# Moving the batch-end sums of a fused attention, Fourier and feed-forward kernel between engines, with a tile of their own for the spread reciprocals

## The chip, the core and the metric

The kernel runs on one core of a Trainium2 chip. The core has five engines that run beside each other and meet at semaphores: TensorE (PE in the profile; PEld is its weight load), VectorE (DVE), ScalarE (ACT), GpSimd (POOL) and SyncE (SP), which here only starts transfers. Each takes its own instructions strictly in their order. The metric is the device time of one launch in microseconds.

## The reference, cut to what matters

Four batches of 576 rows; attention with 8 heads of 64 channels and a decay that is a running sum of logarithms; then the real part of a two-dimensional Fourier transform, added to its input; then a normalisation and a feed-forward pair; then a mixing stage with sines and cosines.

```python
scores = scale * q @ k.T + (cum[:, None] - cum[None, :])      # causal
attn = exp(scores - max); attn = attn / (attn.sum(-1) + 1e-9)
x = (attn @ v)                                                # 4 x 576 x 512
u = x + real(fft(fft(x, axis=1), axis=2))
x = u + relu(norm(u) @ w_ch1) @ w_ch2
theta = x @ w_theta
y = w_tok_r @ (x * cos(theta)) + w_tok_i @ (x * sin(theta))
u = x + y;  out = u + relu(u @ w_ch)
```

Products are done in a reduced format with each operand split into a high part and a low part, so that most tensors exist twice ("hi" and a low part, "kl", "el", "ol" and so on): a copy makes the high part, a subtraction the low part.

## The kernel before, in words

Phase 1 (`phase1`) walks over 32 heads, two of a batch's eight to a pair, four pairs to a batch. For head n+1 it computes scores (`score_units`: two matmuls into a bank, L232 on the high part and L233 on the low parts kl and the query copy q2; a fused VectorE reduction L241 that adds the mask and finds the lowest value; an exponential on ScalarE, L246). For head n it turns the probabilities (`turn_units`: transposes L271 into four banks, copied to PT at L274, bank 0 by VectorE and banks 1 to 3 by ScalarE). For head n+2 it prepares the operands (`prep_units`: ScalarE makes hi at L206, GpSimd the two low parts at L209 and L211 and the query copy at L213). After both heads of a pair come the product with v (`av_units`, L303, into a bank pair T) and the reciprocals of the row sums, turned by TensorE (`spread`, L283) and copied by ScalarE to a tile R (L285, L287).

`evac_pair` multiplies T by R. Before, R is the tile X for an even pair and the tile Y for an odd one (Y shares its memory with ol), and the product overwrites it. After each odd pair rows of Y are shifted by transfers through a small tile, and then the sum E = X + Y (L348) and the difference O = X - Y (L350) are formed: once in the middle of each batch (pair 1) and once at its end (pair 3). With the batch's end, `fft_units` follows: ee (L377) and oo (L381) fold E and O, ScalarE makes eh and oh, then el (L384) and ol (L386) are the low parts; matmuls L406, L417 and L429 with the tables in `dft`; and u at L446 and L447. This runs as filler in the steps of later heads; for the last batch it runs at the start of phase 2.

Phase 2 is the feed-forward pair (L745, L759) over six column blocks and sixteen weight groups; phase 3 the mixing stage. Weights arrive packed and are decoded by ScalarE and VectorE (`decode`, scratch tile a of the tag sq); phase 3 takes its z tiles from the same memory (`z_tile`).

The order on each engine of phase 1 is set by a scheduler that runs ahead of time: it takes the instructions in program order, with matmuls of the scores and of the product with v preferred (`high_priority`), and fixes one list for each engine. From the fifth column block of phase 2 on the order is the program's own.

Of the kernel before, what the change touches and what calls it, by code (L numbers as in the profile page):

```python
# [18 lines left out]
NP = 4  # L19
# [32 lines left out]
def f(ap):  # L52
    return ap.bitcast(F32)


class Net:
# [138 lines left out]
    def prep_units(self, n, pair, raw, hd):  # L195
        nc = self.nc
        g = n % 2
        kl, q2 = pair["kl"], self.q2[g]
        hi = self.w2.tile([128, 2, S], F32R, tag="hi", name="hi")
        hd["hi"] = hi  # L200
        if n == 0:
            nc.scalar.copy(hi[:, 1], raw[:, 1])
            nc.scalar.copy(hi[:, 0], raw[:, 0])
            nc.scalar.copy(q2[0:64], raw[0:64, 1])
        else:
            nc.scalar.copy(hi, raw)  # L206
        yield
        lows = nc.vector if n == 0 else nc.gpsimd
        lows.tensor_tensor(hi[64:128, 1], raw[64:128, 1], f(hi[64:128, 1]), ALU.subtract)  # L209
        yield  # L210
        lows.tensor_tensor(kl[0:64, g], raw[0:64, 0], f(hi[0:64, 0]), ALU.subtract)  # L211
        if n:
            nc.gpsimd.tensor_scalar(q2[0:64], raw[0:64, 1], 1.0, 1.0, ALU.mult, ALU.mult)  # L213
        yield
# [43 lines left out]
    def turn_units(self, hd):  # L258
        nc = self.nc
        P = hd["P"]  # L260
        PT = self.w3.tile([128, 1600], F32, tag="PT", name="PT", bufs=4)
        hd["PT"], hd["copies"] = PT, []
        for bank, pieces in enumerate(TURNED):
            ps = self.bank_b()
            for j, a, b, off in pieces:
                for i in range(5):
                    if TOP[i] + 128 <= a or TOP[i] >= b:
                        continue
                    o = off + TOP[i] - a
                    src = P[:, POFF[i] + TOP[j] : POFF[i] + TOP[j] + 128]  # L270
                    nc.tensor.transpose(ps[:, o : o + 128], src, self.ident)  # L271
            w = TWIDE[bank]
            dst = PT[:, PTOFF[bank] : PTOFF[bank] + w]
            copy = nc.scalar.copy(dst, ps[:, 0:w]) if bank else nc.vector.tensor_copy(dst, ps[:, 0:w])  # L274
            hd["copies"].append(copy)
            yield

    def spread(self, p, T, wide):
        nc = self.nc
        R = self.c1.tile([128, S], F32, tag="ol" if p % 2 else "X", name="Y" if p % 2 else "X", bufs=1)  # L280
        for ps, some in ((self.bank_b(), range(4)), (self.bank_a(), (4,))):
# [41 lines left out]

    def evac_pair(self, p, R, T):
        nc = self.nc
        k = p // 2
        if p % 2 == 0:
            self.X = R
            nc.vector.tensor_tensor(R, T[:, 256:832], R, ALU.mult)
            if k == 0:  # L330
                self.EO = [self.c1.tile([128, 2, S], F32, tag=x, name=x, bufs=2) for x in ("E", "O")]
            return
        X, (E, O) = self.X, self.EO
        Y = R
        nc.vector.tensor_tensor(Y, T[:, 256:832], R, ALU.mult)
        if k == 0:
# [9 lines left out]
        for _ in range(4):  # L346
            yield
        nc.vector.tensor_tensor(E[:, k], X, Y, ALU.add)  # L348
        yield
        nc.vector.tensor_tensor(O[:, k], X, Y, ALU.subtract)  # L350
        yield

    def fft_units(self, b, E, O, rows):
# [5 lines left out]
        for _ in rows:  # L359
            pass  # L360
        ee = w.tile([128, 2, 290], F32, tag="ee", name="ee", bufs=1)
        oo = w.tile([128, 2, 288], F32, tag="oo", name="oo", bufs=1)
# [13 lines left out]
        yield  # L376
        nc.vector.tensor_tensor(ee[:, :, 1:288], E[:, :, 1:288], E[:, :, 575:288:-1], ALU.add)  # L377
        nc.scalar.copy(ee[:, :, 0:289:288], E[:, :, 0:289:288])
        nc.scalar.copy(eh, ee)
        yield  # L380
        nc.vector.tensor_tensor(oo[:, :, 0:287], O[:, :, 1:288], O[:, :, 575:288:-1], ALU.subtract)  # L381
        nc.scalar.copy(oh, oo)
        yield
        (nc.gpsimd if 0 >> (b == B - 1) & 1 else nc.vector).tensor_tensor(el, ee, f(eh), ALU.subtract)  # L384
        yield
        (nc.vector if 3 >> (b == B - 1) & 1 else nc.gpsimd).tensor_tensor(ol, oo, f(oh), ALU.subtract)  # L386
        for _ in range(4):
# [44 lines left out]
        for t in range(2):  # L432
# [12 lines left out]
            nc.vector.scalar_tensor_tensor(oa[:, 289:576], O[:, t, 289:576], -0.5, ps[:, 287:0:-1], ALU.mult, ALU.subtract)  # L445
            (nc.vector if b == B - 1 or 1 >> t & 1 else nc.gpsimd).tensor_tensor(u[:, t, :], ea, oa, ALU.subtract)  # L446
            nc.gpsimd.tensor_tensor(u[:, 2 + t, :], ea, oa, ALU.add)  # L447
            for _ in range(1 if b == B - 1 or t else 7):
# [7 lines left out]
    def phase1(self):  # L456
# [16 lines left out]
        def done(m, T, R):  # L473
            nonlocal rows, fft
            for _ in rows:
                pass
            rows = self.evac_pair(m % NP, R, T)
            next(rows, 0)
# [62 lines left out]
    def decode(self, src, n, place=None, keep=None):  # L541
# [7 lines left out]
        yield  # L549
        a = w.tile([128, 512], F32, tag="sq", name="a", bufs=6)[:, 0:n]  # L550
        if keep is None:
# [338 lines left out]
    def z_tile(self):  # L890
        k = self.nz % 7
        self.nz += 1
        if k < 6:
            return self.x1.tile([128, 2, 256], F32R, tag="sq", name="z", bufs=6)
        return self.q3.tile([128, 2, 256], F32R, tag="z", name="z", bufs=1)

# [290 lines left out]
```

## Time and profile before

| | us |
|---|---|
| median of 3 runs | 980.65 (980.25 to 983.48) |
| profiled execution | 979.22 |
| its span, first to last instruction | 977.5 |
| PE busy | 910.4 (93%) |
| DVE busy | 620.3 (63%) |
| ACT busy | 431.1 (44%) |
| POOL busy | 330.8 (34%) |

The shares are means over three phases with different limits: phase 1 ends at about 290 us, phase 2 at about 700 us. In the page's 40 slices TensorE's busy tenths are 9 in every slice from the 17th to the 39th, and 4 to 9 ahead of them. In a row of the profile a line number is that of the kernel before; the names are those of the program, output first. "PEclk" is the clock granted to TensorE as a share of full speed (2.4 GHz; its lower level is 1.2 GHz, a share of 0.5).

### The profile page before, as it was taken

To read this page: it belongs to the slowest core of one execution; us is meant where nothing else is said; L and a number is where in the kernel's file an instruction comes from. 1 tells how busy PE (TensorE), PEld (TensorE's weight loads), DVE (VectorE), ACT (ScalarE), POOL (GpSimd) and SP (SyncE) were. 2 spreads that over 40 slices of the span, in tenths; PEclk is the share of its full clock that TensorE was granted. 3 is DMA by queue.
4 is the path that set the end of the run, shared out by engine and by line. 5 is a ranking of instruction groups with operands and counts; after the bars stand their busy time and mean duration, and the time that the engine had idled before them with its cause. 6 is when DMAs were issued, how large, how long until landed. Compare 5 with 4: busy or idle time off the path is not lost.

```text
span 977.5 us, 15831 instructions
## 1 busy us (share of the span) xinstructions
PE 910.4 (93%) x5960; PEld 855.0 (87%) x5960; DVE 620.3 (63%) x1464; ACT 431.1 (44%) x1038; POOL 330.8 (34%) x385
## 2 busy tenths in 40 slices
PE   4889898987978998999999999999999999999998
PEld 3677776776757898999999999999999999999998
DVE  7666667576669787625665366626677765746554
ACT  5888668667554343312322133213335543525331
POOL 6867467467531253300000000000014744525330
PEclk9999899988988799999999999999999999999999
DMA  4643232222022212001223122232420000000001
GB/s 144 198 156 102 87 101 88 91 73 88 15 84 68 65 65 66 1 1 45 86 87 118 55 87 87 89 130 92 144 68 1 1 14 37 2 37 14 25 26 49
DMA packets 24337, 68.04 MB, mean 70 GB/s; under 512 B 3535, under 2 KB 6991, under 8 KB 24261
## 3 DMA queue, kind: packets, MB, share of 16 engines
q1 hardware_dynamic: 20420, 62.52, 19.7%
q0 software_dynamic: 3120, 3.33, 1.3%
q10 hardware_dynamic: 720, 1.18, 0.4%
q8 instruction: 47, 0.77, 0.3%
q14 instruction: 30, 0.24, 0.1%
HBM read 57.92 MB, written 9.07 MB: 69 GB/s over the span
## 4 chain that ended last, share of the span: by engine, by line
PE 68%; DVE 15%; ACT 7%; POOL 5%; issue 4%; DMA 2%; SPq 0%; ACTq 0%; POOLq 0%; DVEq 0%
PE pa L745 19%; PE pb L759 11%; PE po L759 8%; PE pb L966 5%; PE pa L977 4%; PE pa L930 4%; PE pt L303 3%; PE po L966 3%; PE pb L271 2%; PE pa L232 2%; ACT P L246 2%; PE pa L233 2%; ACT hi L206 1%; DVE P L241 1%; PE pb L429 1%
## 5 line engine op out<-in xcount | busy, mean ns | idle before, releaser
L745 PE MATMUL pa<-un,wf 128*128 128x384 f32 x1152 | 222.0, 340 | 5.1 <-ACT un L733 3.2
L745 PEld LDWEIGHTS pa<-un,wf 128*128 128x128 f32 x1152 | 203.8, 191 | 7.8 <-ACT un L733 3.9
L751 DVE SCALAR_TENSOR_TENSOR h<-pa,h 128x384 fp32r<-128x384 f32 x96 | 53.2, 555 | 145.6 <-ACT h L750 145.5
L759 PE MATMUL pb<-h,wf 128*128 128x384 f32 x660 | 135.2, 337 | 0.3 <-DVE u L767 0.3
L759 PEld LDWEIGHTS pb<-h,wf 128*128 128x128 f32 x660 | 117.0, 189 | 0.6 <-DVE u L767 0.6
L750 ACT ACTIVATE h<-pa 128x384 fp32r<-128x384 f32 x96 | 46.8, 489 | 154.7 <-PE pa L745 154.6
L246 ACT ACTIVATE P<-P,mn 128x256 f32<-128x256 f32 (+4 forms) x160 | 95.7, 601 | 40.9 <-DVE mn L241 40.7
L241 DVE CUSTOM_DVE_ANT_0 P<-pa,mask 128x256 f32<-128x256 f32 (+4 forms) x160 | 78.3, 512 | 55.5 <-PE pa L233 45.4
L759 PE MATMUL po<-h,wf 128*128 128x384 f32 x492 | 104.4, 340 | 1.1 <-DVE u L767 0.8
L232 PE MATMUL pa<-hi 128*128 128x448 f32 (+2 forms) x192 | 73.6, 396 | 27.7 <-DVE mn L241 11.9
L922 POOL COPY xd<-u 128x64 f32<-128x64 f32 x32 | 6.7, 251 | 272.0 <-DVE u L767 263.8
L966 PE MATMUL pb<-wtk,z 128*128 128x288 f32 x513 | 97.0, 294 | 0.0
L271 PE MATMUL pb<-ident,P 128*128 128x128 f32 x480 | 86.1, 292 | 9.4 <-ACT PT L274 6.2
L759 PEld LDWEIGHTS po<-h,wf 128*128 128x128 f32 x492 | 87.3, 189 | 2.8 <-ACT a L558 1.1
L956 POOL TENSOR_TENSOR z<-kra,z 128x256 fp32r<-128x256 f32 x72 | 53.8, 767 | 86.8 <-ACT z L955 86.8
L966 PEld LDWEIGHTS pb<-wtk,z 128*128 128x128 f32 x513 | 79.2, 188 | 0.0
L966 PE MATMUL po<-wtk,z 128*128 128x288 f32 x351 | 75.1, 295 | 1.1 <-POOL z L956 1.1
L271 PEld LDWEIGHTS pb<-ident,P 128*128 128x128 f32 x480 | 60.6, 148 | 17.0 <-ACT PT L274 9.1
L233 PE MATMUL pa<-kl,q 66*128 66x448 f32 (+2 forms) x192 | 67.1, 372 | 7.0 <-POOL kl L211 3.9
L232 PEld LDWEIGHTS pa<-hi 128*128 128x128 f32 x192 | 39.6, 209 | 37.5 <-DVE mn L241 15.4
L930 PE MATMUL pa<-wf,xs 128*128 128x256 f32 x456 | 63.9, 289 | 0.0
L966 PEld LDWEIGHTS po<-wtk,z 128*128 128x128 f32 x351 | 57.4, 188 | 1.7 <-POOL z L956 1.5
(203 smaller groups left out, 1692.7 us busy)
## 6 DMA issues: line engine op xcount, KB each, us to landing
raw<-in_qk SPq DMA_DIRECT2D x31, 576.0 KB, 3.9
raw<-in_wf SPq DMA_DIRECT2D x32, 512.0 KB, 3.5
raw<-in_wtk SPq DMA_DIRECT2D x18, 288.0 KB, 2.8
v<-in_vp SPq DMA_DIRECT2D x16, 320.0 KB, 3.5
out<-ob SPq DMA_DIRECT2D x12, 288.0 KB, 2.1
dft<-in_dft POOLq DMA_DIRECT2D x8, 346.0 KB, 5.0
raw<-in_wth SPq DMA_DIRECT2D x4, 512.0 KB, 4.6
st_wth<-raw SPq DMA_DIRECT2D x4, 512.0 KB, 5.0
```

What stands on the lines that cost most here:

```text
L232: nc.tensor.matmul(t[:, 0 : b - a], hi[:, 1, q], hi[:, 0, a:b], start=True, stop=False)
L233: nc.tensor.matmul(t[:, 0 : b - a], q2[:, q], kl[:, g, a:b], start=False, stop=True)
L241: nc.vector.tensor_tensor_reduce(out=p[:, a:b], in0=t[:, 0 : b - a], in1=self.mask[:, S - n0 - 128 + a : S - n0 - 128 + b], scale=-0.125, ...
L246: nc.scalar.activation(p, p, AF.Exp, bias=lowest, scale=-1.0, accum_out=zs[:, g, i : i + 1])
L271: nc.tensor.transpose(ps[:, o : o + 128], src, self.ident)
L745: nc.tensor.matmul(ps[:, 0:CH], t[:, l, 128 * d : 128 * d + 128], un[r][:, d], start=n == 0, stop=n == 11)
L750: nc.scalar.activation(h[:, 0], ps[:, 0:CH], AF.Relu)
L751: nc.vector.scalar_tensor_tensor(h[:, 1], ps[:, 0:CH], 0.0, f(h[:, 0]), ALU.max, ALU.subtract)
L759: nc.tensor.matmul(outs[d], t[:, l, 128 * d : 128 * d + 128], h[:, r], start=k % G == 0 and n == 0, stop=k % G == G - 1 and n == 2,)
L930: nc.tensor.matmul(th, xs[:, l, d], self.wth[d][:, r, 256 * hf : 256 * hf + 256], start=n == 0, stop=n == 11)
L956: nc.gpsimd.tensor_tensor(z[:, 1], t, f(z[:, 0]), ALU.subtract)
L966: nc.tensor.matmul(acc[k][th], z[:, l, 128 * k : 128 * k + 128], self.wtk[kt][:, r, 288 * th : 288 * th + 288], start=first and i == 0 and ...
```

## The change

1. `spread` writes to a tile R of its own, and `evac_pair` writes its product to X or Y, instead of multiplying in place.
2. In `evac_pair` E and O go from VectorE to GpSimd, except at the end of the last batch; a step of the schedule is put in behind each.
3. In `fft_units` ee, oo, el, ol and both u go through one name, `two`: GpSimd for the first three batches, VectorE for the last. Before, ee, oo, el and ol were VectorE's in all batches, L446 VectorE's at t = 0 and GpSimd's at t = 1 (VectorE's twice in the last batch), L447 GpSimd's in all.
4. The query copy q2 goes from GpSimd to ScalarE for all heads but the first, where it was there already, and stands before the low parts.
5. Bank 1 of the turned probabilities is copied by VectorE instead of ScalarE.
6. To make room, `decode` has 5 scratch tiles a instead of 6; z tiles come 5 from that memory and 2 from another instead of 6 and 1.

```diff
         else:
             nc.scalar.copy(hi, raw)
         yield
+        nc.scalar.copy(q2[0:64], raw[0:64, 1])
         lows = nc.vector if n == 0 else nc.gpsimd
         lows.tensor_tensor(hi[64:128, 1], raw[64:128, 1], f(hi[64:128, 1]), ALU.subtract)
         yield
         lows.tensor_tensor(kl[0:64, g], raw[0:64, 0], f(hi[0:64, 0]), ALU.subtract)
-        if n:
-            nc.gpsimd.tensor_scalar(q2[0:64], raw[0:64, 1], 1.0, 1.0, ALU.mult, ALU.mult)
         yield
...
-            copy = nc.scalar.copy(dst, ps[:, 0:w]) if bank else nc.vector.tensor_copy(dst, ps[:, 0:w])
+            copy = nc.scalar.copy(dst, ps[:, 0:w]) if bank > 1 else nc.vector.tensor_copy(dst, ps[:, 0:w])
...
     def spread(self, p, T, wide):
-        R = self.c1.tile([128, S], F32, tag="ol" if p % 2 else "X", name="Y" if p % 2 else "X", bufs=1)
+        R = self.c1.tile([128, S], F32, tag="R", name="R", bufs=1)
...
-    def evac_pair(self, p, R, T):
+    def evac_pair(self, p, R, T, last):
         nc = self.nc
         k = p // 2
-        if p % 2 == 0:
-            self.X = R
-            nc.vector.tensor_tensor(R, T[:, 256:832], R, ALU.mult)
+        odd = p % 2
+        Z = self.c1.tile([128, S], F32, tag="ol" if odd else "X", name="Y" if odd else "X", bufs=1)
+        nc.vector.tensor_tensor(Z, T[:, 256:832], R, ALU.mult)
...
-        nc.vector.tensor_tensor(E[:, k], X, Y, ALU.add)
-        yield
-        nc.vector.tensor_tensor(O[:, k], X, Y, ALU.subtract)
+        sums = nc.vector if last else nc.gpsimd
+        sums.tensor_tensor(E[:, k], X, Y, ALU.add)
+        yield
+        yield
+        sums.tensor_tensor(O[:, k], X, Y, ALU.subtract)
+        yield
         yield
...
+        two = nc.vector if b == B - 1 else nc.gpsimd
...
-        nc.vector.tensor_tensor(ee[:, :, 1:288], E[:, :, 1:288], E[:, :, 575:288:-1], ALU.add)
+        two.tensor_tensor(ee[:, :, 1:288], E[:, :, 1:288], E[:, :, 575:288:-1], ALU.add)
...
-        nc.vector.tensor_tensor(oo[:, :, 0:287], O[:, :, 1:288], O[:, :, 575:288:-1], ALU.subtract)
+        two.tensor_tensor(oo[:, :, 0:287], O[:, :, 1:288], O[:, :, 575:288:-1], ALU.subtract)
...
-        (nc.gpsimd if 0 >> (b == B - 1) & 1 else nc.vector).tensor_tensor(el, ee, f(eh), ALU.subtract)
-        yield
-        (nc.vector if 3 >> (b == B - 1) & 1 else nc.gpsimd).tensor_tensor(ol, oo, f(oh), ALU.subtract)
+        two.tensor_tensor(el, ee, f(eh), ALU.subtract)
+        yield
+        two.tensor_tensor(ol, oo, f(oh), ALU.subtract)
...
-            (nc.vector if b == B - 1 or 1 >> t & 1 else nc.gpsimd).tensor_tensor(u[:, t, :], ea, oa, ALU.subtract)
-            nc.gpsimd.tensor_tensor(u[:, 2 + t, :], ea, oa, ALU.add)
+            two.tensor_tensor(u[:, t, :], ea, oa, ALU.subtract)
+            two.tensor_tensor(u[:, 2 + t, :], ea, oa, ALU.add)
...
-            rows = self.evac_pair(m % NP, R, T)
+            rows = self.evac_pair(m % NP, R, T, m == B * NP - 1)
...
-        a = w.tile([128, 512], F32, tag="sq", name="a", bufs=6)[:, 0:n]
+        a = w.tile([128, 512], F32, tag="sq", name="a", bufs=5)[:, 0:n]
...
-        if k < 6:
-            return self.x1.tile([128, 2, 256], F32R, tag="sq", name="z", bufs=6)
-        return self.q3.tile([128, 2, 256], F32R, tag="z", name="z", bufs=1)
+        if k < 5:
+            return self.x1.tile([128, 2, 256], F32R, tag="sq", name="z", bufs=5)
+        return self.q3.tile([128, 2, 256], F32R, tag="z", name="z", bufs=2)
```

The instruction lists show where the parts land. First VectorE at the end of the first batch, before; "ISA P,mn" is the reduction with the mask, "ISA mn" its result being read out, "COPY PT" a bank of turned probabilities, rz_98 the reciprocals:

```order
L241 ISA mn 128x1
L348 TENSOR_TENSOR E<-X,Y 128x576
L350 TENSOR_TENSOR O<-X,Y 128x576
L249 RECIPROCAL rz_98<-rz_98 128x10
L377 TENSOR_TENSOR ee<-E 128x2x287
L381 TENSOR_TENSOR oo<-O 128x2x287
L274 COPY PT<-pb 128x512
L241 ISA P,mn<-pa,mask 128x384
L241 ISA mn 128x1
L384 TENSOR_TENSOR el<-ee,eh 128x580
```

The same place on VectorE in the changed kernel (its line numbers are two lower here):

```order
L239 ISA P,mn<-pa,mask,mn 128x128
L239 ISA mn 128x1
L239 ISA P,mn<-pa,mask 128x512
L239 ISA mn 128x1
L247 RECIPROCAL rz_98<-rz_98 128x10
L272 COPY PT<-pb 128x512
L239 ISA P,mn<-pa,mask 128x384
L239 ISA mn 128x1
L239 ISA P,mn<-pa,mask 128x256
```

The four sums that stood between the reductions for the 512 and the 384 columns are gone from VectorE, and only the reciprocal and a copy stand there. GpSimd at the same place, before (xl a small low part for the transform, "DMA kl" a transfer of the decay's rows, wide the reciprocals spread over columns, q_99 and q_100 the two query copies):

```order
L373 TENSOR_TENSOR xl<-xx,xh 1x290
L369 MEMSET xx 1x2
L186 DMA kl<-scr 2x2x576
L209 TENSOR_TENSOR hi<-raw,hi 64x576
L211 TENSOR_TENSOR kl<-raw,hi 64x576
L213 TENSOR_SCALAR q_100<-raw 64x576
L252 TENSOR_SCALAR wide<-rz_98 128x640
L213 TENSOR_SCALAR q_99<-raw 64x576
L209 TENSOR_TENSOR hi<-raw,hi 64x576
L211 TENSOR_TENSOR kl<-raw,hi 64x576
```

And after:

```order
L209 TENSOR_TENSOR hi<-raw,hi 64x576
L211 TENSOR_TENSOR kl<-raw,hi 64x576
L250 TENSOR_SCALAR wide<-rz_98 128x640
L347 TENSOR_TENSOR E<-X,Y 128x576
L350 TENSOR_TENSOR O<-X,Y 128x576
L379 TENSOR_TENSOR ee<-E 128x2x287
L383 TENSOR_TENSOR oo<-O 128x2x287
L386 TENSOR_TENSOR el<-ee,eh 128x580
L388 TENSOR_TENSOR ol<-oo,oh 128x576
L209 TENSOR_TENSOR hi<-raw,hi 64x576
L211 TENSOR_TENSOR kl<-raw,hi 64x576
```

Six sums now stand on GpSimd in one block between the low parts of one head and those of the next, and the query copies are gone from it. At the end of the third batch GpSimd's list in the changed kernel is another one:

```order
L186 DMA kl<-scr 2x2x576
L347 TENSOR_TENSOR E<-X,Y 128x576
L350 TENSOR_TENSOR O<-X,Y 128x576
L375 TENSOR_TENSOR xl<-xx,xh 1x290
L379 TENSOR_TENSOR ee<-E 128x2x287
L383 TENSOR_TENSOR oo<-O 128x2x287
L250 TENSOR_SCALAR wide<-rz_98 128x640
L209 TENSOR_TENSOR hi<-raw,hi 64x576
L211 TENSOR_TENSOR kl<-raw,hi 64x576
L386 TENSOR_TENSOR el<-ee,eh 128x580
L371 MEMSET xx 1x2
L388 TENSOR_TENSOR ol<-oo,oh 128x576
```

There the next head's low parts stand ahead of el and ol.

## Rows read from the trace of the kernel before

**Rows 1.** Busy time in stretches: us, PE, PEld, DVE, ACT, POOL, PEclk, DMA share, GB/s

```profile
20.00:290.00 270.00, 234.92 (x1652) 190.09 (x1651) 174.48 (x536) 191.95 (x529) 166.47 (x175) 0.94 0.31 97
65.00:75.00 10.00, 7.92 (x46) 6.73 (x47) 7.39 (x22) 8.04 (x27) 5.51 (x6) 0.83 0.47 152
95.00:110.00 15.00, 11.65 (x72) 8.42 (x70) 10.69 (x26) 8.87 (x24) 7.28 (x6) 0.77 0.31 92
125.00:135.00 10.00, 8.57 (x64) 7.21 (x61) 8.13 (x23) 5.67 (x17) 6.52 (x6) 1.00 0.30 94
160.00:175.00 15.00, 11.55 (x58) 8.16 (x60) 12.87 (x28) 11.92 (x33) 10.69 (x10) 0.77 0.26 90
200.00:210.00 10.00, 8.06 (x38) 7.27 (x39) 8.70 (x21) 5.88 (x19) 6.35 (x6) 0.66 0.20 61
235.00:250.00 15.00, 11.29 (x69) 9.27 (x68) 9.41 (x21) 8.16 (x24) 6.86 (x5) 0.77 0.18 56
```

**Rows 2.** Waits, 20 to 290 us: engine, tile, line <- releaser: us, times, longest

```profile
PE pa L232 <- DVE mn L241: 9.8, 12, 2.1
PE pa L232 <- ACT X L285: 4.3, 3, 3.4
PE pa L233 <- POOL q L213: 1.8, 2, 1.0
```

**Rows 3.** Timeline of the first mid-batch sums: start, us, engine, line, operation [idle before]

```profile
64.71 0.76 DVE L348 TENSOR_TENSOR E<-X,Y 128x576 f32<-128x576 f32 x1 [0.17 <-POOL Y L340]
65.33 1.39 POOL L209 TENSOR_TENSOR hi<-raw,hi 64x576 fp32r<-64x576 f32 x1
65.39 1.96 DVE L350 TENSOR_TENSOR O<-X,Y 128x576 f32<-128x576 f32 x1
66.80 1.81 POOL L211 TENSOR_TENSOR kl<-raw,hi 64x576 fp32r<-64x576 f32 x1
67.61 0.33 PE L232 MATMUL pa<-hi 128*128 128x128 f32 x1 [2.08 <-DVE mn L241]
73.00 0.37 PE L233 MATMUL pa<-kl,q 66*128 66x448 f32 x1
```

**Rows 4.** Groups of instructions by line and form: count | busy us, mean ns | idle before

```profile
L350 DVE TENSOR_TENSOR O<-X,Y 128x576 f32<-128x576 f32 x8 | 11.3, 1412 | 0.0
L348 DVE TENSOR_TENSOR E<-X,Y 128x576 f32<-128x576 f32 x8 | 7.4, 920 | 2.3 <-DMA Y<-x 2.1 <-POOL Y L340 0.2
L377 DVE TENSOR_TENSOR ee<-E 128x574 f32<-128x574 f32 x4 | 3.5, 862 | 0.0
L381 DVE TENSOR_TENSOR oo<-O 128x574 f32<-128x574 f32 x4 | 3.6, 912 | 0.0
L384 DVE TENSOR_TENSOR el<-ee,eh 128x580 fp32r<-128x580 f32 x4 | 3.0, 753 | 0.1
L386 DVE TENSOR_TENSOR ol<-oo,oh 128x576 fp32r<-128x576 f32 x4 | 4.1, 1015 | 0.0
L446 DVE TENSOR_TENSOR u<-ea,oa 128x576 f32<-128x576 f32 x5 | 7.4, 1479 | 0.0
L446 POOL TENSOR_TENSOR u<-ea,oa 128x576 f32<-128x576 f32 x3 | 4.3, 1430 | 2.2 <-DVE oa L445 2.2
L213 POOL TENSOR_SCALAR q<-raw 64x576 fp32r<-64x576 f32 x31 | 23.1, 746 | 24.4 <-PE pa L233 23.9 <-DMA raw<-in_qk 0.4
L274 DVE COPY PT<-pb 128x512 f32<-128x512 f32 x32 | 21.7, 680 | 2.9 <-PE pb L271 2.8
```

**Rows 5.** Groups by line and form: bank copies on ScalarE and waits of the transposes

```profile
L274 ACT COPY PT<-pb 128x512 f32<-128x512 f32 x32 | 18.4, 575 | 14.7 <-PE pb L271 14.5
L271 PE MATMUL pb<-ident,P 128*128 128x128 f32 x480 | 86.1, 292 | 9.4 <-ACT PT L274 6.2 <-ACT X L287 1.6 <-DVE uc L702 0.4
```

**Rows 6.** Timeline at the end of the third batch

```profile
236.02 0.90 DVE L348 TENSOR_TENSOR E<-X,Y 128x576 f32<-128x576 f32 x1 [1.76 <-DMA Y<-x]
...
240.45 0.80 PE L406 MATMUL pb<-dft,eh 128*128 128x258 f32 x2
```

More of the change, by code (lines that the diff above doesn't have):

```diff
@@ L203, in prep_units @@
             nc.scalar.copy(hi[:, 0], raw[:, 0])
-            nc.scalar.copy(q2[0:64], raw[0:64, 1])
         else:
@@ L322, in av_units @@
         done(m, T, R)
-    def evac_pair(self, p, R, T):
+    def evac_pair(self, p, R, T, last):
         nc = self.nc
         k = p // 2
-        if p % 2 == 0:
-            self.X = R
-            nc.vector.tensor_tensor(R, T[:, 256:832], R, ALU.mult)
+        odd = p % 2
+        Z = self.c1.tile([128, S], F32, tag="ol" if odd else "X", name="Y" if odd else "X", bufs=1)
+        nc.vector.tensor_tensor(Z, T[:, 256:832], R, ALU.mult)
+        if not odd:
+            self.X = Z
             if k == 0:
@@ L332, in evac_pair @@
             return
-        X, (E, O) = self.X, self.EO
-        Y = R
-        nc.vector.tensor_tensor(Y, T[:, 256:832], R, ALU.mult)
+        X, Y, (E, O) = self.X, Z, self.EO
         if k == 0:
```

## The prediction

> **What bounds the kernel now.** I read the busy shares by slice first. TensorE fills nearly every slice after phase 1 and is the bound there, so the change can matter only in phase 1 and in the last batch's transform behind it. The table of stretches comes second [rows 1]. From 20 to 290 us TensorE is busy 234.92 of 270 us, so 35 us are idle, and VectorE, ScalarE and GpSimd each stand at 62 to 71% of the stretch: no engine is full, the work waits in turns. The loss is not spread evenly. Six stretches, 75 us together, hold the sums E and O: three in the middle of a batch (from 65, 125 and 200 us) and three at its end (from 95, 160 and 235 us). They take 46, 64, 38 and 72, 58, 69 matmuls, 347 in all. The other 195 us take 1652 - 347 = 1305, or 6.7 in a us. At that rate the 347 would need 52 us, so the six stretches lose about 23 us: 7.9 us in the mid-batch ones (30 us less 148/6.7) and 15.3 us at the ends (45 us less 199/6.7). Matmuls differ in width, so this is an estimate good to a few us. The same rows show how: in five of the six the mean granted clock is 0.66 to 0.83, so part of each ran at 1.2 instead of 2.4 GHz after TensorE had idled.
>
> Third, what TensorE waits for [rows 2]. The largest waits of its score matmuls are for the lowest value from VectorE, 9.8 us in 12 times, and for ScalarE's copy of the spread reciprocals, 4.3 us in 3. The timeline of the first mid-batch sums shows the mechanism [rows 3]. E takes 0.76 us, O 1.96 us, and the reduction queued behind O comes 2 us late; TensorE idles 2.08 us until it is there. GpSimd was making the low parts hi and kl at the time. By its mean (1412 ns) O is the sum that suffers most [rows 4]; 0.76 us is what one costs undisturbed. ScalarE's copy waits because, before, its target is the tile X, which E and O must have read first.
>
> **The change part by part.** All prices are of one profiled execution of 979.22 us (977.5 us of span and 1.7 around it); it lies 1.4 us under the median of the runs.
>
> Sums. From VectorE go 7 of 8 E (0.92), 7 of 8 O (1.41), 3 each of ee, oo, el, ol (0.862 + 0.912 + 0.753 + 1.015) and 3 of L446 (1.48): 6.4 + 9.9 + 10.6 + 4.4 = 31.3 us [rows 4]. GpSimd takes the same 29 at about 1.43 us, the price of its own L446: 41.5 us. The query copies leave it: 23.1 us of work and 24.4 us of idling in front of them, since each had to wait until TensorE had read the copy before [rows 4]. GpSimd so goes from 166 to about 185 of 270 us.
>
> Mid-batch. E and O are wanted only at the batch's end, so on GpSimd they are in nobody's way but the next low parts'. Two cost 2.9 us; kl ended at 68.61 and was read at 73.00, a margin of 4.4 us [rows 3]. I count 80% of the 7.9 us as won: 6.3. Ends: none of it to all of it.
>
> Batch end. Here the sums lie on a chain that TensorE waits for: E, ee, eh, el, then L406. On VectorE the chain blocks the reductions; on GpSimd it is a block of six, 8.6 us, ahead of the next low parts, and el comes 5 x 1.43 = 7.2 us after E could start. In the first two batches TensorE has scores, transposes or the product with v to fill part of that. I take half of these two stretches' loss (30 us less 130/6.7 is 10.6): 5.3. In the third batch the list puts the next low parts ahead of el: from E's start at 236.0 us six more two-input instructions and E itself, 7 x 1.43 = 10.0 us, make el no earlier than 246.0, where TensorE came to L406 at 240.45 [rows 6]. The new wait of up to 5.6 us eats that stretch's 4.7 us: I count 0 (bounds -0.9 to +4.7).
>
> The Trainium skill (GPSIMD Engine Reference, section 4.1, Engine selection) speaks against this part: elementwise work with two inputs belongs on VectorE, GpSimd being about 2 times slower. The trace agrees, 1430 against 760 ns [rows 3, 4]; by that rule alone the chain at a batch end gets longer and the place is lost, which is the third rival below. Another page (SBUF — State Buffer, section Who interferes with whom) says that a VectorE instruction with two inputs there and a GpSimd instruction reading there hold the shared pair one at a time, each blocking the other whole. O fits it: started at 65.39, beside hi from 65.33 to 66.72, it ended 0.63 us after hi did [rows 3]. By that rule the whole 7.9 us mid-batch are won and the sum below is 1.6 us larger.
>
> Query copies. TensorE waited 1.8 us for them [rows 2]; I count that as won. On ScalarE one costs between 0.575 us (a 512-column copy [rows 5]) and 0.746 us (GpSimd's own [rows 4]); I take 0.66, so 31 add 20.5 us, and bank 1 takes 18.4 away: +2.1 us on an engine busy 192 of 270 us. What stands behind a query copy is an exponential that TensorE's transposes want. The scheduler puts the copy behind the exponentials of the head whose scores last read that tile, so it should find it free. Cost 0 to 2.1, I take 1.0.
>
> Bank 1. VectorE gets 32 x 0.680 = 21.8 us, so it is 9.5 us lighter in all; each copy comes 0.1 us later than on ScalarE, 3.4 us if every one counted, against 6.2 us for which the transposes waited on ScalarE's copies [rows 5]. Between -6.2 and +3.4, I take 0: TensorE's transposes run a bank ahead.
>
> R of its own. The copies wait no more for E and O; the 4.3 us of rows 2 lie inside the stretches above and are not counted again.
>
> Last batch. Two L447 come to VectorE (2 x 0.76), and its two L446, 1.48 on the mean with GpSimd beside them, may fall to 0.76: 1.5 against 1.4, so 0. Scratch tiles: at most two raw loads are open at a time, and ScalarE's and VectorE's decoding lies under a full TensorE; 0, and up to 1 us if that cover fails.
>
> Sum: -6.3 - 5.3 - 1.8 + 1.0 = -12.4 us, 966.8 for an execution like the profiled one, 968.2 beside the median. I predict 968 us.
>
> **The rivals.** A, everything comes back: the batch ends too, because the waiting matmuls find fill. Then -23.2 - 1.8 + 1.0 = -24.0, 957 us. For it: VectorE is what TensorE waits for most [rows 2]. Against: 8.6 us in one block.
>
> B, the waits move on: GpSimd or ScalarE hold TensorE for as long as VectorE did, and the net lies within 3 us of 980.6. For it: three helpers at 62 to 71%. Against: the mid-batch sums have no reader for many us.
>
> C, slower: GpSimd becomes late at the three batch ends. TensorE stands at el and, behind it in its order, the next scores and product. Each end would cost the 8.6 us of the block and some 3.4 us of slow clock behind it (0.23 of 15 us, as in the rows of the ends): 36 us in place of the 15.3 now, +20.7, less the 7.1 won elsewhere (6.3 + 1.8 - 1.0): +13.6 at the worst. It decides from where an end costs (15.3 + 7.1 + 2.9)/3 = 8.4 us, that is, when TensorE finds next to nothing to fill with. I put it at +8: 989 us.
>
> **How the numbers follow.** The forecast 0.58, A 0.17, B 0.12, C 0.13. What a measurement of this kernel can tell from no change is 0.3%, 2.9 us. The forecast and A are faster by more: 0.75; B is the same: 0.12; C slower: 0.13. The forecast's own range is 960 to 977 (mid-batch all to half, ends of the first two batches all to none). The range that takes in A's upper half, B and C's lower end is 955 to 985.
>
> **What would show it.** In the changed profile no VectorE sum stands between two reductions in the first three batches; E, O and their followers are GpSimd's at 1.40 to 1.45 us, and the low parts fall back to about 1.41. The mid-batch stretches run at full clock with no wait of TensorE over 1 us. A wait of L406 for GpSimd's el appears at the third batch's end, several us long, and shorter ones at the first two. Phase 1 ends some 12 us earlier and the rest keeps its length. I am wrong if the waits for el or for kl add up to more than 15 us, if the score matmuls wait for ScalarE's query copy in many heads, or if phase 1 gets shorter and phase 2 gives it back.

## The result, and the profile after

The changed kernel takes 970.93 us in the median of six runs (969.71 to 974.46), the kernel before 980.45 us (978.71 to 983.48, six runs). The ratio is 0.9906, with a 95% interval from 0.9883 to 0.9928: 9.2 us less, where 12.4 less and 968 us were predicted. The total came out near the forecast; its parts did not, as the experiments show.

The profiled execution of the changed kernel took 972.97 us (span 971.2, clock 0.975). It lies 2.0 us above its median, that of before 1.2 us under the one of its six runs, so this pair of traces shows 6.3 of the 9 us. Phase 1, up to the end of the last matmul of the product with v, ends at 282.33 us instead of 286.98, 4.7 us earlier; what follows is 1.6 us shorter.

First the stretches, to be held against [rows 1]. They lie where the sums now run: three at the same times as there, three 1 to 11 us earlier. Columns as there.

```profile
20.00:290.00 270.00, 233.90 (x1659) 187.08 (x1658) 167.15 (x549) 195.37 (x535) 182.03 (x176) 0.94 0.32 99
65.00:75.00 10.00, 8.42 (x48) 6.54 (x48) 6.93 (x24) 8.61 (x28) 7.10 (x7) 0.85 0.48 153
124.00:134.00 10.00, 9.98 (x76) 7.98 (x77) 5.85 (x21) 5.98 (x18) 8.47 (x8) 1.00 0.31 94
189.00:199.00 10.00, 9.96 (x76) 7.67 (x74) 5.70 (x19) 5.65 (x18) 7.66 (x7) 1.00 0.33 95
95.00:110.00 15.00, 10.42 (x57) 7.91 (x57) 6.23 (x20) 9.87 (x27) 13.35 (x11) 0.77 0.12 40
160.00:175.00 15.00, 10.77 (x60) 7.32 (x60) 6.44 (x23) 10.32 (x29) 13.23 (x12) 0.77 0.18 60
225.00:240.00 15.00, 8.20 (x45) 7.07 (x45) 5.04 (x20) 8.76 (x28) 13.85 (x13) 0.74 0.32 101
```

The three mid-batch stretches hold 200 matmuls where 148 stood before, and two of them run at full clock with TensorE all but never idle. The three batch ends hold 162 where 199 stood, GpSimd is full there (13.2 to 13.9 of 15 us), and the clock is at 0.74 to 0.77 (0.77 in all three before). By the prediction's own measure of 6.7 matmuls in a us the mid-batch loss falls from 7.9 us to 0.1, and the loss at the ends rises from 15.3 to 20.8.

Then the waits from 20 to 290 us (engine, tile, line <- releaser: us, times, longest). The first six rows are TensorE's and answer to [rows 2]; the last two are ScalarE's and VectorE's.

```profile
PE pa L230 <- POOL hi L209: 6.3, 2, 5.3
PE pa L231 <- POOL kl L211: 4.3, 5, 1.4
PE pa L231 <- ACT q L207: 3.9, 1, 3.9
PE pa L230 <- DVE mn L239: 3.3, 3, 2.6
...
PE pb L408 <- POOL xx L371: 1.5, 1, 1.5
PE pb L408 <- POOL el L386: 0.5, 1, 0.5
...
ACT ee L380 <- POOL ee L379: 10.5, 3, 4.1
DVE X L327 <- POOL O L350: 5.7, 2, 2.9
```

The wait for the lowest value fell from 9.8 us to 3.3 and the one for X is gone. In their place stand GpSimd's low parts and ScalarE's query copy. The two last rows are new: ScalarE stands 10.5 us at the edge copy of ee (four elements, L380), and VectorE 5.7 us at the product X of the next pair (L327), which goes to the tile that O still reads. The timeline of the first batch end shows what stands behind them (start, us, engine, line, operation [idle before]).

```profile
97.34 1.40 POOL L347 TENSOR_TENSOR E<-X,Y 128x576 f32<-128x576 f32 x1
98.71 1.39 POOL L350 TENSOR_TENSOR O<-X,Y 128x576 f32<-128x576 f32 x1
100.06 1.39 POOL L379 TENSOR_TENSOR ee<-E 128x574 f32<-128x574 f32 x1
100.12 0.76 DVE L327 TENSOR_TENSOR X<-pt,R 128x576 f32<-128x576 f32 x1 [2.85 <-POOL O L350]
...
101.49 0.20 ACT L380 COPY ee<-E 128x4 f32<-128x4 f32 x1 [3.56 <-POOL ee L379]
101.59 0.67 ACT L207 CAST q<-raw 64x576 fp32r<-64x576 f32 x1
...
102.40 1.15 PE L231 MATMUL pa<-kl,q 66*128 66x448 f32 x3 [3.92 <-ACT q L207]
```

The query copy needs nothing of the sums. It stood behind the edge copy in ScalarE's order, so TensorE stood 3.92 us for it. At the third end it is GpSimd's own order.

```profile
226.33 1.43 POOL L347 TENSOR_TENSOR E<-X,Y 128x576 f32<-128x576 f32 x1
...
232.58 0.72 POOL L250 TENSOR_SCALAR wide<-rz 128x640 f32<-128x640 f32 x1
...
233.38 1.40 POOL L209 TENSOR_TENSOR hi<-raw,hi 64x576 fp32r<-64x576 f32 x1
...
234.83 0.85 PE L230 MATMUL pa<-hi 128*128 128x448 f32 x2 [5.35 <-POOL hi L209]
...
236.22 1.40 POOL L386 TENSOR_TENSOR el<-ee,eh 128x580 fp32r<-128x580 f32 x1
237.68 0.58 PE L408 MATMUL pb<-dft,el 128*128 128x258 f32 x1 [1.46 <-POOL xx L371]
```

The low part hi came only behind E, O, xl, ee, oo and wide, and TensorE stood 5.35 us for it. The 1.46 us after it are the wait for el: the memset that is named as releaser was queued right behind el, which ended at 237.6.

Last the groups of moved instructions, against [rows 4, 5] (count | busy us, mean ns | idle before).

```profile
L350 POOL TENSOR_TENSOR O<-X,Y 128x576 f32<-128x576 f32 x7 | 9.9, 1413 | 0.0
L386 POOL TENSOR_TENSOR el<-ee,eh 128x580 fp32r<-128x580 f32 x3 | 4.2, 1412 | 0.2 <-ACT eh L381 0.2
L207 ACT CAST q<-raw 64x576 fp32r<-64x576 f32 x32 | 21.4, 668 | 0.0
L272 DVE COPY PT<-pb 128x512 f32<-128x512 f32 x64 | 43.6, 682 | 16.7 <-PE pb L269 16.4
```

The prices were those predicted: 1.41 us for a sum on GpSimd, 0.668 for a query copy, 0.68 for a bank. What was wrong is what the pieces are worth where they stand.

### The profile page after: what moved, and what is told of

It is laid out like the page before. It is cut to its first block, busy times and chain, and to the rows that moved or that the text cites. A ratio compares the mean times of both kernels' runs of the same rounds, so it can differ in the third digit from the quotient of the medians.

```text
span 971.2 us, 15852 instructions
## 1 busy us (share of the span) xinstructions
PE 906.7 (93%) x5960; PEld 849.4 (87%) x5960; DVE 605.8 (62%) x1469; ACT 430.9 (44%) x1037; POOL 337.4 (35%) x381
## 4 chain that ended last, share of the span: by engine, by line
PE 58%; DVE 10%; ACT 3%; DMA 2%; issue 1%; POOL 1%; ACTq 0%; DVEq 0%; SPq 0%; POOLq 0%
PE pa L747 18%; PE pb L761 11%; PE po L761 8%; PE pb L968 5%; PE pa L979 4%; PE pa L932 4%; PE po L968 3%; DMA raw<-in_wf 1%; DVE kra L939 1%; DVE kra L956 1%; DVE kra L942 1%; DVE a L567 1%; DVE a L565 1%; PE pb L431 1%; DVE kra L941 1%
## 5 line engine op out<-in xcount | busy, mean ns | idle before, releaser
L244 ACT ACTIVATE P<-P,mn 128x512 f32<-128x512 f32 (+4 forms) x160 | 95.5, 600 | 37.7 <-DVE mn L239 37.3
L239 DVE CUSTOM_DVE_ANT_0 P<-pa,mask 128x448 f32<-128x448 f32 (+4 forms) x160 | 77.5, 510 | 51.9 <-PE pa L231 43.9
L230 PE MATMUL pa<-hi 128*128 128x448 f32 (+2 forms) x192 | 70.8, 386 | 24.3 <-ACT hi L205 11.0
L269 PE MATMUL pb<-ident,P 128*128 128x128 f32 x480 | 82.8, 285 | 5.7 <-ACT PT L272 2.1
L231 PE MATMUL pa<-kl,q 66*128 66x448 f32 (+2 forms) x192 | 64.1, 362 | 8.5 <-POOL kl L211 4.3
L269 PEld LDWEIGHTS pb<-ident,P 128*128 128x128 f32 x480 | 57.8, 145 | 11.8 <-issue 2.7
L230 PEld LDWEIGHTS pa<-hi 128*128 128x128 f32 x192 | 38.0, 203 | 33.1 <-issue 11.9
L209 POOL TENSOR_TENSOR hi<-raw,hi 64x576 fp32r<-64x576 f32 x31 | 44.1, 1424 | 43.7 <-ACT hi L205 25.3
```

Of the source, the lines that this page charges most:

```text
L230: nc.tensor.matmul(t[:, 0 : b - a], hi[:, 1, q], hi[:, 0, a:b], start=True, stop=False)
L231: nc.tensor.matmul(t[:, 0 : b - a], q2[:, q], kl[:, g, a:b], start=False, stop=True)
L239: nc.vector.tensor_tensor_reduce(out=p[:, a:b], in0=t[:, 0 : b - a], in1=self.mask[:, S - n0 - 128 + a : S - n0 - 128 + b], scale=-0.125, ...
L244: nc.scalar.activation(p, p, AF.Exp, bias=lowest, scale=-1.0, accum_out=zs[:, g, i : i + 1])
```

## The experiments

Every kernel ran in turn with the kernel before on one chip. A difference in us below is the ratio's difference from 1, or between two ratios, times 980.4 us; the band given with it is the root of the summed squares of the two half intervals.

| run | what it is | median us | ratio, 95% interval |
|---|---|---|---|
| mid_only | changed, ends' six sums on VectorE | 962.21 | 0.9818 [0.9791, 0.9845] |
| ends_only | changed, mid-batch E, O on VectorE | 976.87 | 0.9970 [0.9954, 0.9986] |
| edge_gpsimd | changed, edge copy of ee on GpSimd | 970.77 | 0.9909 [0.9887, 0.9932] |
| x_two | changed, two tiles X in place of R | 971.67 | 0.9916 [0.9885, 0.9946] |
| no_sums | changed, all six sums on VectorE | 962.86 | 0.9842 [0.9818, 0.9866] |
| r_only | before, with R | 978.48 | 0.9987 [0.9972, 1.0001] |
| bank1_scalar | changed, bank 1 on ScalarE | 973.09 | 0.9944 [0.9924, 0.9965] |
| q_gpsimd | changed, query copies on GpSimd | 988.65 | 1.0101 [1.0079, 1.0123] |
| q_only | before, query copies on ScalarE | 974.30 | 0.9943 [0.9923, 0.9964] |
| q_three | before, a third query tile | 983.57 | 1.0039 [1.0024, 1.0053] |
| ends_eo | changed, only ee, oo, el, ol of the ends on VectorE | 965.95 | 0.9854 [0.9838, 0.9870] |
| no_sums_bank1 | no_sums, bank 1 on ScalarE | 974.30 | 0.9934 [0.9908, 0.9960] |

**mid_only: only the mid-batch sums on GpSimd.**

```diff
-        sums = nc.vector if last else nc.gpsimd
+        sums = nc.vector if k else nc.gpsimd
-        two.tensor_tensor(ee[:, :, 1:288], ...   # and oo, el, ol
+        nc.vector.tensor_tensor(ee[:, :, 1:288], ...
```

> The changed kernel, but at the batch ends E, O, ee, oo, el and ol are VectorE's again; GpSimd keeps the mid-batch E and O, and both u. Theory: the gain of 9.5 us comes from the mid-batch sums, and the batch ends now cost more than before, because ScalarE and VectorE stand in their queues for GpSimd's block (10.5 us in 3 at the edge copy of ee, 5.7 us in 2 at the product X); with the block gone about 4 us more are won: 967 us. Rival 1, the prediction's split (6.3 mid-batch, 5.3 batch ends): the ends' gain goes back, 976 us. Rival 2, neither place matters and the moved copies made the gain: 971 us as the whole change.

962.21 us: 8.6 us (± 3.5) less than the whole change. The theory's direction holds, with twice its size: with the other parts in place, the sums of the batch ends lose time on GpSimd, and the prediction's 5.3 us won there are refuted. With no_sums below, from which it cannot be told apart, it is the fastest of all kernels tried.

**ends_only: only the ends' sums on GpSimd.**

```diff
-        sums = nc.vector if last else nc.gpsimd
+        sums = nc.vector if last or k == 0 else nc.gpsimd
```

> The changed kernel, but the mid-batch E and O are VectorE's again in all batches; the batch ends stay on GpSimd. Theory: the mid-batch gain of some 9 us goes, 980 us, as before the change. Rival 1, the prediction's split: 6.3 us go back, 977 us. Rival 2, the moved copies made the gain: 971 us.

976.87 us: 6.3 us (± 2.7) go back, the size that the prediction had for the mid-batch sums. But 2.9 us of gain are left although the ends lose, so the moved copies must gain, and more than the theory gave them.

**edge_gpsimd and x_two: each takes away one of the two new stalls.**

```diff
-        nc.scalar.copy(ee[:, :, 0:289:288], E[:, :, 0:289:288])
+        two.tensor_copy(ee[:, :, 0:289:288], E[:, :, 0:289:288])
```

> The changed kernel, but the four-element edge copy into ee is taken from ScalarE to GpSimd in the first three batches, so that nothing of ScalarE's stands behind GpSimd's ee but eh itself; in the first two batches ScalarE's list is otherwise the same. Theory: the query copy and the exponentials behind the edge copy come up to 4 us earlier at each batch end; TensorE's 3.9 us for the query copy at the first end goes and some of the 1.6 us for a bank copy at the second: 966 us, and the profile shows no wait of ScalarE for ee of over 1 us ahead of a query copy. Rival: GpSimd's block of six is itself what binds, since the low parts hi and kl stand behind it, and ScalarE's eh waits for ee just as long: 971 us.

```diff
-        R = self.c1.tile([128, S], F32, tag="R", name="R", bufs=1)
+        R = self.c1.tile([128, S], F32, tag="ol" if p % 2 else "X", name="Y" if p % 2 else "X", bufs=1 if p % 2 else 2)
...
-        Z = self.c1.tile([128, S], F32, tag="ol" if odd else "X", name="Y" if odd else "X", bufs=1)
-        nc.vector.tensor_tensor(Z, T[:, 256:832], R, ALU.mult)
+        Z = R
+        nc.vector.tensor_tensor(Z, T[:, 256:832], R, ALU.mult)
```

> The changed kernel, but the memory of R goes into a second tile X: the reciprocals are copied into X or Y and multiplied in place, and X has two tiles, so that the product of the next pair need not wait until GpSimd has read the old X for O. Theory: VectorE's 5.7 us in 2 waits at the product X go, and with them TensorE's 2.6 us for the lowest value queued behind it at the second batch end; 968 us. Rival: VectorE's wait is covered, since ScalarE's stall at the edge copy holds the same heads: 971 us.

970.77 and 971.67 us: no difference from the changed kernel in either. The theory that either of the two queues, taken by itself, makes the loss falls; both rivals stand. No run takes both stalls away at once. The waits of edge_gpsimd from 20 to 290 us, TensorE's and then ScalarE's, show where it went.

```profile
PE pa L230 <- POOL hi L209: 6.4, 2, 5.5
PE pb L408 <- ACT eh L381: 4.3, 1, 4.3
...
ACT eh L381 <- POOL ee L380: 13.4, 3, 5.1
```

The query copy now comes in time; ScalarE stands instead at eh, which needs ee itself, and TensorE at eh. The wait for GpSimd's hi is as in the changed kernel. In x_two VectorE's stall for O is gone, and TensorE's waits are those of the changed kernel, with one for a bank that has grown from 2.1 to 4.8 us:

```profile
PE pa L230 <- POOL hi L209: 6.3, 2, 5.4
PE pb L269 <- ACT PT L272: 4.8, 2, 4.2
PE pa L231 <- ACT q L207: 3.9, 1, 3.9
```

**ends_eo: a shorter block.** The edit is that of mid_only without its first two lines.

> The changed kernel with ee, oo, el and ol on VectorE again at all batch ends, while E and O stay on GpSimd there too (GpSimd's block is two instructions, 2.8 us, in place of six, 8.6 us). Theory: what costs at the ends is the length of the block ahead of the next low parts and in front of eh; with a third of it a third of the cost is left: between 962 (no E and O there) and 971 (all six), 965 us. Rival: the start of the chain on GpSimd is what costs, since VectorE's ee and product X queue behind O there: 971 us.

965.95 us, 1 us from the expectation: E and O alone cost 3.5 us (± 3.1) at the ends, the four behind them 5.1 more (± 2.7). The size fits the theory that the block's length costs. TensorE's waits from 20 to 290 us say that it is not the whole of it:

```profile
PE pa L231 <- ACT q L207: 3.9, 1, 3.9
...
PE pa L230 <- POOL wide L250: 2.7, 1, 2.7
...
PE pa L230 <- POOL hi L209: 0.9, 1, 0.9
```

The wait for the low part hi shrank with the block, from 6.3 us to 0.9 (2.7 for wide stand beside it). The 3.9 us for the query copy stayed whole at the first end: VectorE's ee still has to wait for E on GpSimd, and the copy stands behind it on ScalarE, as the rival has it. In these waits the next low parts suffer from the length of the block and the query copy from the chain's start on GpSimd; how the 8.6 us divide between the two is not shown.

**no_sums: none of the six sums moved.** The edit is that of mid_only with `sums = nc.vector`.

> The changed kernel with all of E, O, ee, oo, el and ol on VectorE again, mid-batch and batch end; what is left of the change is R, the query copies on ScalarE, bank 1 on VectorE and u on GpSimd. Theory: the two places add up, so by the two runs that each kept one (962.2 and 976.9) and the whole (970.9) this kernel takes 962.2 + 976.9 - 970.9 = 968 us, and the other parts alone gain about 11 us, which the prediction had at 0.8 beside the waits for X. Rival 1, the prediction's prices: 1.8 won, 1.0 lost, of the waits for X some 2 to 4 won: 976 us. Rival 2: without the relief by the sums VectorE is too full for bank 1's 21.8 us: 980 us or more.

962.86 us, 15.5 us under the kernel before, and all of it from the parts other than the six sums: the query copies, bank 1, R, the u, and the added steps of the schedule. The prediction had them at 0.8 us, beside the waits for X that it counted with the sums. Neither the u nor the added steps were run by themselves. The two places do not add up: the mid-batch sums on GpSimd are worth 2.4 us (± 3.5, none of it certain) while the ends stand on VectorE, and 6.3 with the ends on GpSimd.

**r_only, bank1_scalar, q_gpsimd: one part each.**

```diff
-        R = self.c1.tile([128, S], F32, tag="ol" if p % 2 else "X", ...   # r_only, on the kernel before, with the scratch tiles
+        R = self.c1.tile([128, S], F32, tag="R", name="R", bufs=1)
...
-            copy = nc.scalar.copy(dst, ps[:, 0:w]) if bank > 1 else ...   # bank1_scalar, on the changed kernel
+            copy = nc.scalar.copy(dst, ps[:, 0:w]) if bank else ...
...
-        nc.scalar.copy(q2[0:64], raw[0:64, 1])                            # q_gpsimd, on the changed kernel, but for head 0
+            nc.gpsimd.tensor_scalar(q2[0:64], raw[0:64, 1], 1.0, 1.0, ALU.mult, ALU.mult)
```

> The kernel before with the tile R of its own and the smaller scratch memory alone; all sums and copies stay where they were before. Theory: the 4.3 us that TensorE waited for ScalarE's copy into X, and the 7.9 us that ScalarE stood there for O, go: 974 us. Rival: the copies are early enough and VectorE's sums hold the same heads: 979 us. The scratch memory is expected at 0 in both.

978.48 us: 1.3 us, at the edge of what can be told from nothing; the rival holds. TensorE's 4.3 us for X went, and a wait of 4.8 us for eh took their place.

> The changed kernel with bank 1's copy on ScalarE again. Theory: with the sums gone from VectorE the copy is earlier there, and ScalarE, which stands at batch ends for GpSimd, is lighter by 18.4 us; the transposes' wait for banks, 6.2 us before and 2.1 after, comes back: 975 us. Rival, the prediction's 0: 971 us.

973.09 us: 3.7 us (± 3.0) lost, the theory's sign. The transposes' wait for ScalarE's copies came back, as it said (6.2 us), and TensorE's wait for hi, of which it said nothing, rose from 6.3 to 15.7 us.

> The changed kernel with the query copies on GpSimd again. Theory: GpSimd's block at the batch ends is what binds, and 31 x 0.75 us more on it, each copy behind TensorE's reading of the copy before, make the low parts later still: 978 us or more. Rival, the prediction's 0.8 us for this part: 972 us.

988.65 us: 19.1 us lost, slower than the kernel before. With both the sums and the query copies on GpSimd TensorE waits 11.9 us in 7 for the copies, as its waits from 20 to 290 us show; that is part of the loss, and the rest of it is not traced.

```profile
PE pa L234 <- POOL q L214: 11.9, 7, 4.6
PE pa L233 <- DVE mn L242: 6.4, 8, 2.6
PE pa L233 <- POOL hi L210: 4.9, 4, 1.6
```

**q_only and q_three: why the query copies matter.**

```diff
+        nc.scalar.copy(q2[0:64], raw[0:64, 1])     # q_only, on the kernel before
-        if n:
-            nc.gpsimd.tensor_scalar(q2[0:64], raw[0:64, 1], 1.0, 1.0, ALU.mult, ALU.mult)
...
-        kl, q2 = pair["kl"], self.q2[g]            # q_three, on the kernel before
+        kl, q2 = pair["kl"], self.q2[n % 3]
```

> The kernel before with the query copies on ScalarE alone; nothing else is changed. Theory: this part is the whole gain of some 15 us that the other runs leave for it (putting it back cost 17.7 us, the kernel without any moved sums gained 17.4 us, R alone 1.3, bank 1 about 2): 966 us. Rival 1, the prediction's price of 0.8 us: 979 us. Rival 2: ScalarE, which here keeps bank 1 as well, gets too full with 20 us more, and the copies pay only together with bank 1 on VectorE: 973 us or more.

974.30 us: 5.6 us won. Neither the theory's 14 nor the prediction's 0.8; the second rival's size.

> The kernel before with a third tile for the query copy (heads take them in turn) and the smaller scratch memory that makes room for it; the copies stay on GpSimd, with the same work. Tells apart why the copies cost what they cost there. Theory 1, the wait: before, a copy had to wait until TensorE had read the copy two heads back, 23.9 us in 10, and the next head's low parts stood behind it on GpSimd; with a third tile that wait goes and with it most of the loss: 968 us. Theory 2, the work: 31 x 0.75 us stand ahead of low parts however early their tile is free: 979 us.

983.57 us, 3.8 us slower. GpSimd's waits from 20 to 290 us:

```profile
POOL q L214 <- DMA raw<-in_qk: 30.2, 14, 3.9
...
POOL q L214 <- PE pa L234: 5.6, 2, 3.2
```

The group of the copies (count | busy us, mean ns | idle before), to be held against that of L213 in [rows 4]:

```profile
L214 POOL TENSOR_SCALAR q<-raw 64x576 fp32r<-64x576 f32 x31 | 23.3, 750 | 36.2 <-DMA raw<-in_qk 30.4 <-PE pa L234 5.6
```

The wait for TensorE fell from 23.9 us to 5.6 and nothing was won: theory 1's 968 us are refuted. Its mechanism is not, because GpSimd did not stop standing at the copies. In its list all 31 now stood ahead of their own head's low parts (23 before) and waited for its data instead, and the idle time in front of the copies rose from 24.4 us to 36.2. Besides, the end of phase 1 came only 1.2 us later than before (288.19 against 286.98 us); the rest of the loss lies behind it, where no query copy runs, and its cause is not traced (r_only has the same smaller scratch memory and lost at most 0.4 us there). Theory 2's figure is the nearer one, but no run here takes the work away and leaves the copies on GpSimd, so it is not shown either.

**no_sums_bank1: bank 1, with the query copies on ScalarE.**

> As no_sums (all six sums on VectorE, R of its own, query copies on ScalarE), but bank 1's copy on ScalarE again. Theory: the query copies and bank 1 pay together, because ScalarE takes 20.5 us and gives 18.4 away; the query copies alone gained 5.6 us and R alone 1.3, so this kernel stands near 980.4 - 6.9 = 973.5 us, and bank 1 is worth some 8.6 us on top of them. Rival: bank 1 is worth what putting it back in the whole change cost, 3.7 us, here too: 968.5 us, and the rest of the gain of no_sums is the joint effect of R and the query copies.

974.30 us, as the theory has it. Beside query copies on ScalarE bank 1 on VectorE is worth 9.0 us (± 3.5). TensorE's waits up to its own end of phase 1, first here and then in no_sums, show by what:

```profile
PE pa L230 <- DVE mn L239: 11.5, 9, 4.1
PE pb L269 <- ACT PT L272: 7.0, 10, 1.2
PE pb L269 <- ACT R L285: 3.2, 4, 1.3
```

```profile
PE pa L230 <- DVE mn L239: 5.7, 6, 1.6
...
PE pb L269 <- ACT PT L272: 1.6, 4, 0.5
```

The waits for ScalarE's banks fall by 5.4 us (those for VectorE's banks grow from 0.2 to 2.2), but those for the lowest value, an instruction of VectorE, fall by 5.8 as well, although VectorE got 21.8 us more to do.

## Why the prediction was right in sum and wrong in its parts

One way through the runs splits the 9.2 us; another order of the same steps would give other shares, since they do not add up.

| step | predicted us | measured us | from |
|---|---|---|---|
| query copies (with R, the u and the added steps) | -0.8 | -6.5 | before to no_sums_bank1 |
| bank 1 | 0 (-6.2 to +3.4) | -9.0 | no_sums_bank1 to no_sums |
| mid-batch sums | -6.3 | -2.4 | no_sums to mid_only |
| batch-end sums | -5.3 | +8.6 | mid_only to changed |
| sum | -12.4 | -9.2 | |

That the sum came out so near is luck: the terms missed by 5.7, 9.0, 3.9 and 13.9 us, and the misses all but cancelled.

*What bounds the kernel.* Right: the work waits in turns, and most of the time came and went in phase 1. Right as well that VectorE was the engine waited for. But taking the sums away is not needed to relieve it: in no_sums, with all the sums on VectorE and bank 1 besides, TensorE's wait for the lowest value is 5.7 us, against 9.8 before and 3.3 in the changed kernel.

*Mid-batch.* The mechanism showed itself: no VectorE sum between the reductions, 76 matmuls in 10 us, full clock in two of three places. The first kept a clock of 0.85 and a wait of 1.4 us for kl. The size depends on what else is moved, 6.3 us (± 2.7) or 2.4 (± 3.5). In no_sums E and O still stand between reductions, and TensorE loses less by it than before (last section).

*Batch ends: the step that failed, by sign.* I counted 5 x 1.43 us from E to el and gave TensorE other work for it. The wait for el was short, 0.5 and 1.5 us. What I left out is what stands behind GpSimd's block in the other lists: the next low parts on GpSimd itself, the query copy behind the edge copy on ScalarE, the product X on VectorE. I had asked of the block "who reads el", and not "what stands in every queue that waits for one of the six". Of the rivals it is C, with its place right, its engine right (GpSimd late) and its path wrong, since it had TensorE stand at el: 8.6 us (± 3.5) lost beside the other parts' gain, not enough to turn the sum. The Trainium skill (GPSIMD Engine Reference, section 4.1, Engine selection) keeps elementwise work with two inputs on VectorE; at the batch ends the runs agree, 962.2 against 970.9 us; in mid-batch they show no difference, 962.2 against 962.9.

*Query copies: mis-sized.* I took as their price what TensorE waited for them by name, 1.8 us less 1.0. Alone they gain 5.6 us, and putting them back into the changed kernel costs 19.1. On ScalarE the work was priced rightly, 0.668 us each; the wait for it, 3.9 us in one, is over the 0 to 2.1 us that I allowed, and it comes from the edge copy ahead of it.

*Bank 1: mis-sized.* Its 9.0 us (± 3.5) lie outside my bound of 6.2, though their interval reaches into it. I took the sum of the waits that named these copies, 6.2 us, as the most that could come back. But an engine that is late can also make others late: the exponentials and copies of R stand in ScalarE's list behind a bank, TensorE's transposes behind those, and VectorE's reductions behind TensorE's scores. The waits that name VectorE fell too, which fits this chain; no run tests it by itself.

*Last batch: priced at 0.* Before, the second of the two L447 that went to VectorE took GpSimd 3.41 us and ended 5.2 us after the transform's last matmul (314.93 us). In the changed kernel VectorE does it in 0.74 us and ends 3.3 us after that matmul (310.24 us). First the line of before, then that of the changed kernel:

```profile
316.74 3.41 POOL L447 TENSOR_TENSOR u<-ea,oa 128x576 f32<-128x576 f32 x1 [2.75 <-DVE oa L445]
...
312.75 0.74 DVE L449 TENSOR_TENSOR u<-ea,oa 128x576 f32<-128x576 f32 x1
```

From that matmul to the end the changed kernel's trace is 1.6 us shorter than that of before. The traces of all nine other kernels with the last batch's u on VectorE are shorter there too, by 1.6 to 4.9 us; the three that leave the u where they were (q_only, r_only, q_three) are not. No run moves the u alone, but this is where time was won behind phase 1.

*What a wait does not name.* Part of the rest is in the clock. From 20 us to the end of the last matmul of the product with v:

| | end us | TensorE idle | TensorE busy | mean clock |
|---|---|---|---|---|
| before | 286.98 | 32.9 | 234.1 | 0.94 |
| changed | 282.33 | 31.6 | 230.8 | 0.94 |
| q_only | 281.27 | 29.8 | 231.4 | 0.96 |
| no_sums_bank1 | 285.49 | 32.3 | 233.2 | 0.94 |
| no_sums | 269.88 | 24.1 | 225.8 | 0.98 |
| mid_only | 272.67 | 23.8 | 228.9 | 0.96 |
| q_gpsimd | 299.61 | 41.2 | 238.4 | 0.93 |

The row of no_sums in that view (columns as in [rows 1]):

```profile
20.00:269.88 249.88, 225.79 (x1639) 178.24 (x1638) 182.47 (x557) 188.78 (x521) 145.70 (x146) 0.98 0.33 103
```

Its phase 1 is 17.1 us shorter than before's: 8.8 us less idle time, and 8.3 us less busy time for 1639 matmuls in place of 1647, with the mean clock at 0.98 in place of 0.94. So nearly half of the gain stands in no row of the waits. My sum reckoned with slow clock only inside the six stretches.

*The signs named.* Sums of 1.40 to 1.45 us on GpSimd: 1.39 to 1.42. Low parts at 1.41: 1.42 and 1.41, from 1.45 and 1.49. Phase 1 some 12 us earlier: 4.7. None of the three things that were to prove me wrong came in full: the waits for el and kl make 6.3 us together (12.6 with the low part hi, which I had not named), ScalarE's query copy was waited for once, and phase 2 gave nothing back.

*What stays open.* How the query copies on GpSimd cost 5.6 us is not shown. TensorE's reading of the old copy is not the whole of it: that wait fell by 18.3 us in q_three, with another in its place, and nothing was won. No run moves the sums without the other parts. Each edit also makes the scheduler write new lists for all engines, so steps of 2 or 3 us may be the list's and not the edit's.

## What to carry to other kernels

Before work is moved to an idle engine, list for each of its results every queue in which an instruction waits for it, and what stands behind that instruction; here a block on the idle engine cost 8.6 us although its last result was hardly waited for. The table of waits by releaser is no safe bound for the worth of a relief on either side (4.3 us for X gave 1.3 ± 1.4, 6.2 us for bank 1 gave 9.0 ± 3.5), all the less where the mean clock changes with the idle time. A sum that came out right proves none of its terms: here misses of about 15 us one way (query copies and bank 1) and 18 the other (both places of the sums) made a forecast that was 3 us off, and undoing one part at a time found a kernel (mid_only) that is 8.6 us faster than the change.

## What the runs showed that I had not expected

In no_sums the first mid-batch sums on VectorE, beside GpSimd's low parts, are slower than before, and yet the kernel is the second fastest. Here they are on the timeline:

```profile
63.22 1.41 POOL L209 TENSOR_TENSOR hi<-raw,hi 64x576 fp32r<-64x576 f32 x1
...
63.86 1.38 DVE L347 TENSOR_TENSOR E<-X,Y 128x576 f32<-128x576 f32 x1
...
64.70 1.81 POOL L211 TENSOR_TENSOR kl<-raw,hi 64x576 fp32r<-64x576 f32 x1
...
65.16 1.96 DVE L350 TENSOR_TENSOR O<-X,Y 128x576 f32<-128x576 f32 x1
```

E and O take 3.3 us together where 1.5 is the undisturbed price, O ends 0.6 us behind kl, as it did behind hi in [rows 3], and the low part is stretched to 1.81 us too. The rows go on agreeing with the rule of the Trainium skill that the prediction named (SBUF — State Buffer, Who interferes with whom); but the 7.9 us that were to be won by it are 2.4 (± 3.5) here. One reason is that TensorE lost less at this place: it stood 1.27 us for the lowest value, against 2.08 before, and the clock stayed full in the 10 us around it, where it was 0.83 before.

```profile
62.00:72.00 10.00, 8.47 (x58) 6.77 (x58) 9.68 (x26) 8.58 (x26) 5.07 (x5) 1.00 0.48 153
```

Another is that the lists shifted: in the next two mid-batch places of no_sums E and O take 0.75 to 0.76 us each, undisturbed, while before those of the third took 1.42 and 1.96. So moving other work can take the sums out of the low parts' way, and the sums themselves need not move.
